# Attention and a spectral filter in one statically scheduled kernel: six exp buffers for four, longer rows of value matmuls, column-tile fillers, bf16 filter products

## The chip, the cores and the metric

The kernel runs on one core of one Trainium2 chip. Times are device microseconds (us) from the runs; a span is the time from the first to the last instruction in the trace. TensorE (PE in the profile) multiplies matrices, ScalarE (ACT) computes exponentials, VectorE (DVE) does the rest, SyncE issues transfers. PSUM is the memory that TensorE writes its results to, in eight banks; an eviction is the copy of a result out of it.

## The reference

Two independent layers on inputs of 2048 x 640, their outputs side by side:

```python
# A: spectral filter
X = rfft2(x); X = X * (w_r + 1j*w_i); a = irfft2(X)
# B: attention, 32 heads of 20
q, k, v = heads(x @ wqkv)
p = softmax(q @ k.T * 20**-0.5)
b = (p @ v) @ wo
return concatenate([a, b], axis=-1)
```

The cost is in B: 32 x 2048 x 2048 = 134 million exponentials. The kernel handles them as 2048 tiles of 128 keys by 512 queries. A unit is four heads and 512 queries: 64 tiles; there are 32 units.

## The kernel before

The program of each engine is laid out ahead of time. While the kernel is built, a loop plays through the execution with costs for every operation, and each engine that becomes free takes the first job in its own list of preferences that is ready. What comes out is a fixed order of instructions for each engine with waits on semaphores. The costs in that loop order the instructions and nothing else; on the chip only the order and the waits count. (The kernel holds a second, plain program, class `KB`, that runs only when a check at the end of the first finds its sums out of range.)

```python
def dispatch(self, e):
    if e == "pe":
        return (self.try_qk() or self.try_x_alone() or self.more_bg() or self.try_pv(4)
                or self.tail_pe() or self.try_bg_pe() or self.warm())
    if e == "act":
        if self.try_exp() or self.tail_act(): return True
        ...
    if e == "dve":
        return (self.dve_q(self.dve_urgent) or self.try_bg_ev("dve") or self.try_x_first()
                or self.try_x_step() or self.vmax())
```

- `try_qk`: score matmuls of 3 or 2 tiles, in row tiles of the array, into one of two halves of PSUM (3 + 2 banks).
- `try_exp`: ScalarE exponentiates such a group into one of four exp buffers `PT`, if that buffer is free.
- `try_pv`: value matmuls, four heads at once in column tiles, into PSUM bank 6; when all tiles of a buffer are used, it is free.
- `x`: a tile pair that VectorE exponentiates itself.
- `bg`: all other work, in PSUM banks 5 and 7: projections, out-projection, and the filter's matmuls. `try_bg_ev` moves their results out of PSUM.
- `warm`: filler matmuls of zeros, meant to keep TensorE's clock up.

Row tiles, column tiles and the whole array are the three tiling modes of TensorE. A row of value matmuls is several passes of `try_pv` one after another, with no change of mode between them.

Of the kernel before, what the change touches and what calls it, by code (L numbers as in the profile page):

```python
# [266 lines left out]
class KB:  # L267
# [805 lines left out]
    def mk_jobs_A(self, p0_after):  # L1073
# [171 lines left out]
        for ci_, (b0, n) in enumerate(chunks):  # L1245
            ne = n * 128
            flat = lambda t, c: t[:, c, b0:b0 + n, :].rearrange("p b m -> p (b m)")
            wr, wi, y0, y1 = flat(self.Wp, 0), flat(self.Wp, 1), flat(self.XY, 0), flat(self.XY, 1)
            t = [tt[:, 0:ne] for tt in self.tmp]

            def mult(k, w, ne=ne, t=t):
                def mkev(bank):
                    return lambda e, en: e.tensor_tensor(t[k], ps[:, bank, 0:ne], w, ALU.mult)  # L1253
                return (mkev, 0.0, 1.0417 * ne + 124, kw, [("tmp", k)] + zw("K", 2), [])

            def comb(y, k0, k1, op, key, t=t):
                def mkev(bank):
                    return lambda e, en: e.tensor_tensor(y, t[k0], t[k1], op)
                return (mkev, 0.0, 1.0417 * ne + 144, [("tmp", k0), ("tmp", k1), zr("K", 2)], [key] + zw("B", 3), [])
            for co in range(2):  # L1260
                pe = []
                for ti, (m, ci) in enumerate(((0, 0), (1, 1)) if co == 0 else ((0, 1), (2, 0))):
                    def mk(bank, m=m, ci=ci, b0=b0, n=n, ti=ti):
                        r_ = self.BT[:, ci, b0:b0 + n, :].rearrange("p b m -> p (b m)")
                        return lambda e: e.matmul(ps[:, bank, 0:n * 128], self.kron[:, m, :], r_, start=(ti == 0), stop=(ti == 1))
                    pe.append((mk, ne / 2.4 + 3, [("BT", ci, ci_ // 2), ("kron",), zr("A", 4)]))
                if co == 0:
                    ev = [mult(0, wr), mult(2, wi)]
                    aft = [s5[(0, ci_ // 2)], s5[(1, ci_ // 2)]] + ([s7[ci_ - 1]] if ci_ else st["S4"] + st["S2"])
                else:  # L1270
                    ev = [mult(1, wi), mult(3, wr), comb(y0, 0, 1, ALU.subtract, ("XY", 0, ci_)), comb(y1, 2, 3, ALU.add, ("XY", 1, ci_))]
                    aft = [s7[ci_]]
                s7[ci_] = self.add_job(Job("FS2_%d_%d" % (ci_, co), PRIO, pe, ev, after=aft))
                s7[ci_].ev_eng = "dve"
# [10 lines left out]
        n10 = 8 * 2 * 256  # L1285

        def s10_load(J, p, h=0):
            self.dma(self.iCS.rearrange("p s m n -> p (s m n)"), self.c_iCS.ap()[:, h * n10:(h + 1) * n10], w=[("iCS",)] + zw("K", 3), name="ld_iCS")
        J_s10l = evt("S10load", [s7[nch - 1]], s10_load, lat=8)
        st["S10"] = []  # L1290
        for h in range(2):
            if h:
                J_s10l = evt("S10load1", list(st["S10"]), lambda J, p: s10_load(J, p, 1), lat=8)
            for lt, sp in [(lt, sp) for lt in range(3) for sp in range(4 * h, 4 * h + 4)]:
                M = 128 if lt < 2 else 65
                pe = []
                for i in range(2):
                    sbv = 2 * sp + i
                    for c in range(2):
                        def mk(bank, sbv=sbv, c=c, i=i, lt=lt, M=M):  # L1300
                            o = ps[0:M, bank, i * 256:(i + 1) * 256]
                            l = self.UT[:, sbv, c, lt * 128:lt * 128 + M]
                            r_ = self.iCS[:, sbv % 8, c, :]
                            s_, e_ = (c == 0), (c == 1)
                            return lambda e: e.matmul(o, l, r_, start=s_, stop=e_)
                        pe.append((mk, 108.0, [*[("UT", c, b) for b in range(6)], ("iCS",), zr("B", 4), zr("K", 3)]))
# [8 lines left out]
        def s11_load(J, p):  # L1315
            self.dma(self.G.rearrange("p t c d -> p (t c d)"), self.c_G.ap(), w=[("G",)] + zw("K", 4), name="ld_G")
        J_s11l = evt("S11load", st["S10"], s11_load, lat=8)
        st["S11"] = []
        for sbv in range(16):
            for half in range(2):  # L1320
                pe = []
                n6 = 0
                for lt in range(3):
                    M = 128 if lt < 2 else 65
                    for c in range(2):
                        def mk(bank, lt=lt, c=c, M=M, sbv=sbv, half=half, n6=n6):
                            o = ps[:, bank, 0:320]
                            l = self.ZT[0:M, lt, sbv, c, :]
                            r_ = self.G[0:M, lt, c, half * 320:(half + 1) * 320]
# [39 lines left out]
NXV = 3  # L1369
LOG2E = 1.4426950408889634  # L1370
# [10 lines left out]
class FK(KB):  # L1381
# [8 lines left out]
    def alloc(self):  # L1390
# [12 lines left out]
        self.wq_pad = a.bf(take(10240), 5 * 8 * 128).rearrange("p (c g m) -> p c g m", c=5, g=8)  # L1403
# [3 lines left out]
        self.PT = [a.bf(take(3072 - 1024 * (i % 2)), 1536 - 512 * (i % 2)) for i in range(4)]  # L1407
# [24 lines left out]
    def zone(self, z, total):  # L1432
# [5 lines left out]
        self.spare = total - self.zK - 8192  # L1438
        assert self.zK + 8192 <= total, (self.zK + 8192, total)
# [18 lines left out]
        self.tmp = [a.f32(zK + i * 2048, 512) for i in range(4)]  # L1458
        self.iCS = a.bf(zK, 8 * 2 * 256).rearrange("p (s m n) -> p s m n", s=8, m=2)
        self.G = a.bf(zK, 3 * 2 * 640).rearrange("p (t c d) -> p t c d", t=3, c=2)  # L1460

    def setup_B(self):
# [4 lines left out]
        kq[:, 0] = kq[:, 2] = 1.0  # L1467
        kq[20::32, 0:4] = (0.0, 1.0, 0.0, Y_ROW)
        kqd = self.nc.inline_tensor(kq, self.prefix + "kq")
# [7 lines left out]
        def ldw(a, b, key):  # L1477
            self.dma(self.wqkv[:, :, a:b], wv[:, :, a:b], w=[("wqkv", key)], name="ld_w" + key)
        ldx(0)
        ldw(640, 736, "k0")  # L1480
        ldw(0, 80, "q0")
# [5 lines left out]
        ldw(80, 640, "q")  # L1487
        ldw(1360, 1920, "v")
        wq, ws, zt, va, ps, o1 = self.wq_pad, self.ws, self.zt, self.Vaug, self.ps, self.ones1
# [3 lines left out]
        wq5 = wq.rearrange("p c g (j e) -> p (c g j) e", e=32)[:, :, 20:32]  # L1493
        P.add("dve", lambda e: e.memset(wq5, 0.0), w=[("wqz",)], name="ms_wq")
# [5 lines left out]
        self.wpad("act", 0)  # L1500

    def add_row(self, e, en, out, in_, c):

# [4 lines left out]

    def wpad(self, en, g):

        src = self.wqkv[:, :, g * 80: g * 80 + 80].rearrange("p c (j d) -> p c j d", j=4)
        d4 = self.wq_pad[:, :, g, :].rearrange("p c (j e) -> p c j e", e=32)[:, :, :, 0:20]
        self.P.add(en, lambda e: copy_on(e, en, d4, src), r=[("wqkv", "q" if g else "q0"), ("z", "B", 0)], w=[("wq", g)], name="wpad")
        self.wq_done.add(g)
# [85 lines left out]
    def dummy2(self):  # L1600

        ps, k, z = self.ps, self.KT, self.zt.to_broadcast([128, 128])
        self.P.add("pe", lambda e: e.matmul(ps[:, 6, :], z, k[:, 0, 0:512], start=False, stop=False, skip_group_check=True),  # L1603
                   r=[("KT", 0, 0), ("zt",)], pw=[("ps", 6)], name="dummy")

    def job_QA(self, u):
# [3 lines left out]
        for cbv in range(5):  # L1610
            def mk(bank, cbv=cbv):
                o = ps[:, bank, :]
                l = self.wq_pad[:, cbv, g, :]
                r_ = self.xT[:, cbv, qc * 512:(qc + 1) * 512]
                st, sp = (cbv == 0), (cbv == 4)
                return lambda e: e.matmul(o, l, r_, start=st, stop=sp)  # L1616
            pe.append((mk, 216.0, [("wq", g), ("wqz",), ("xT", qc, cbv // 2)]))

        def mkev(bank):
# [3 lines left out]
        cond = lambda p: g in self.wq_done and (u < 2 or self.qk_left[u - 2] == 0)  # L1623
        return Job("QA%d" % u, 0.0, pe, ev, after=[self.sj[("xT", qc, gi)] for gi in range(3)], cond=cond,
                   minp=(0.0 if u == 0 else 21000.0))
# [98 lines left out]
    def try_exp(self):  # L1724
        i = self.nexp
        if i >= self.nqk or self.qk_t[i] > self.now or self.pt_free[i % 4] > self.now:
# [4 lines left out]
        pt = self.PT[i % 4][:, 0:512 * n]  # L1731
        in_ = self.ps[:, h:h + n, :].rearrange("p b n -> p (b n)")
        self.P.add("act", lambda e: e.activation(pt, in_, AF.Exp, scale=SCALE, bias=-15.0 / LOG2E),  # L1733
                   r=[("ps", h + k) for k in range(n)], w=[("PT", i % 4)], name="exp")
        t = self.occupy("act", 512 * n * 0.8333 + 50.0, 0.0)
        self.half_free[i % 2] = t
        self.pt_free[i % 4] = 1e18
        self.pt_left[i % 4] = n
        for k, (u, kt, j) in enumerate(tiles):
            self.pv_ready[u].append((t, kt, j, self.PT[i % 4][:, 512 * k:512 * k + 512], ("PT", i % 4)))  # L1740
# [8 lines left out]
    def next_x(self, js):  # L1749
# [28 lines left out]
        if tile[2] in js and self.x_skip < 2:  # L1778
# [6 lines left out]
    def try_x_alone(self):  # L1785
        if self.x_pair is None or (self.x_pair[0][0] >= self.u_act and self.now < self.x_at + 2500.0):
# [76 lines left out]
    def try_pv(self, least):  # L1863
# [16 lines left out]
        stuck = i < self.nqk and self.qk_t[i] <= self.now and self.pt_free[i % 4] > self.now + 1e9 and self.tf["act"] <= self.now  # L1880
        if len(pick) < (1 if stuck else min(least, heads)):
            return False

# [32 lines left out]

    def wpad_late(self, g):
        self.wpad("dve", g)
        self.occupy("dve", 350.0)
# [278 lines left out]
    def warm(self):  # L2198
# [8 lines left out]
        self.occupy("pe", self.pe_dur(216.0, "f"))  # L2207
        return True

    def dispatch(self, e):  # L2210
        if e == "pe":
            return (self.try_qk() or self.try_x_alone() or self.more_bg() or self.try_pv(4) or self.tail_pe() or self.try_bg_pe() or self.warm())
# [10 lines left out]
    def run(self):  # L2223
# [17 lines left out]
        self.pt_free = [0.0] * 4  # L2241
        self.pt_left = [0] * 4
# [47 lines left out]
        for g in range(1, NG):  # L2290
            t = 19000.0 + 2000.0 * g
            self.dve_urgent.append((t, lambda g=g: self.wpad_late(g)))
            self.at(t)
# [46 lines left out]
    def build(self):  # L2340
        self.wq_done = set()
# [7 lines left out]
def bass_concat_heads__spectral_gfnet__softmax_full_mha__prompt_kernel(  # L2349
# [11 lines left out]
    fast = FK(nc, arena, *args, cfg=dict(LEAD=20, T_A=760000.0, WARM_SHARE=0.45, RUN=2, PVQ=8, WIN=1400.0, T_X=40000.0, AHEAD=45e3, T_RB=9000.0))  # L2361
# [32 lines left out]
```

## Time and profile before

| | before |
|---|---|
| time, median of the first three runs | 877.55 us (876.75 to 877.59) |
| ScalarE, VectorE, TensorE busy | 95%, 90%, 92% of the span |
| exp groups on ScalarE, polynomial tiles on VectorE | 724, 238 |
| ScalarE idle before exps | 18.8 us |
| VectorE busy from 40 to 820 us | 729.4 of 780 us |

"Idle before, releaser" in a group's row is the time in which the engine stood still just before these instructions and what ended most of it. The prediction below shows the rows for ScalarE. It does not show who kept VectorE waiting while it might have computed polynomials (waits of VectorE from 40 to 830 us: us in total, times, longest):

```profile
DVE arena L1807 <- PE ps L1716: 20.4, 28, 1.4
DVE arena L1507 <- PE ps L1616: 4.3, 5, 1.9
DVE arena L1507 <- PE ps L1548: 3.7, 3, 1.8
DVE arena L227 <- PE ps L1983: 3.3, 2, 1.8
```

L1807 is the polynomial's first step, waiting for its score tile (L1716); the other rows are evictions of query projections, key projections and out-projections. The loop gives VectorE any job that is ready, so a long wait at an eviction suggests that no polynomial step was ready when the order was laid out; it does not prove it, as on the chip the order is fixed.

### The profile page before, as it was taken

To read this page: it belongs to the slowest core of one execution; us is meant where nothing else is said; L and a number is where in the kernel's file an instruction comes from. 1 tells how busy PE (TensorE), PEld (TensorE's weight loads), DVE (VectorE), ACT (ScalarE), POOL (GpSimd) and SP (SyncE) were. 2 spreads that over 40 slices of the span, in tenths; PEclk is the share of its full clock that TensorE was granted. 3 is DMA by queue.
4 is the path that set the end of the run, shared out by engine and by line. 5 is a ranking of instruction groups with operands and counts; after the bars stand their busy time and mean duration, and the time that the engine had idled before them with its cause. 6 is when DMAs were issued, how large, how long until landed. Compare 5 with 4: busy or idle time off the path is not lost.

```text
span 875.8 us, 16211 instructions
## 1 busy us (share of the span) xinstructions
PE 804.7 (92%) x6687; PEld 285.9 (33%) x6772; DVE 785.9 (90%) x1495; ACT 835.2 (95%) x740; POOL 2.9 (0%) x7
## 2 busy tenths in 40 slices
PE   8999999999889999999899988999999999999986
PEld 4433333334233333322233422222333333323322
DVE  3487799999998799999999899999999989999993
ACT  6999999999999899999999999999999999999993
POOL 1000000000000000000000000000000000000000
PEclk9999999999999999999999999999999999999999
DMA  8430000000311000010100000001001120111101
GB/s 239 95 82 14 2 13 14 14 13 3 139 46 37 21 13 2 14 49 14 49 13 30 19 10 14 13 13 51 13 13 63 36 58 11 43 43 44 44 14 33
DMA packets 31972, 31.83 MB, mean 36 GB/s; under 512 B 13588, under 2 KB 26644, under 8 KB 31636
## 3 DMA queue, kind: packets, MB, share of 16 engines
q1 hardware_dynamic: 31892, 30.73, 11.6%
q8 instruction: 54, 0.88, 0.4%
q14 instruction: 26, 0.21, 0.1%
HBM read 24.97 MB, written 5.50 MB: 35 GB/s over the span
## 4 chain that ended last, share of the span: by engine, by line
ACT 55%; DVE 26%; PE 16%; issue 1%; DMA 0%; SPq 0%; ACTq 0%; DVEq 0%
ACT arena L1733 55%; PE ps L1716 5%; DVE arena L227 5%; DVE arena L1807 4%; PE ps L1899 3%; DVE arena L1507 2%; DVE arena L1847 2%; DVE arena L1851 2%; DVE arena L1854 2%; DVE arena L1253 2%; PE ps L1983 1%; DVE arena L2186 1%; DVE arena L1845 1%; DVE arena L1843 1%; DVE arena L1849 1%
## 5 line engine op out<-in xcount | busy, mean ns | idle before, releaser
L1733 ACT ACTIVATE arena<-ps 128x1536 bf16<-128x1536 f32 x724 | 826.0, 1277 | 18.8 <-PE ps L1716 9.3
L1716 PE MATMUL ps<-arena 32*128 32x512 bf16 x2048 | 303.8, 384 | 47.3 <-ACT arena L1733 33.2
L1899 PE MATMUL ps<-arena 128*32 128x512 bf16 (+3 forms) x2048 | 203.1, 390 | 2.9 <-DVE arena L1923 1.7
L1807 DVE TENSOR_SCALAR arena<-ps 128x512 uint16<-128x512 f32 x238 | 163.1, 685 | 21.6 <-PE ps L1716 20.4
L1716 PEld LDWEIGHTS ps<-arena 32*128 32x128 bf16 x2048 | 74.8, 91 | 250.2 <-ACT arena L1733 199.9
L227 DVE CAST arena<-ps 128x320 bf16<-128x320 f32 (+4 forms) x190 | 103.7, 546 | 16.7 <-PE ps L1576 10.1
L1899 PEld LDWEIGHTS ps<-arena 128*32 128x32 bf16 (+1 forms) x2048 | 51.0, 92 | 124.4 <-issue 102.4
L1847 DVE TENSOR_TENSOR arena<-arena 128x1024 f16<-128x1024 uint16 x119 | 81.4, 686 | 1.3
L1851 DVE TENSOR_TENSOR arena<-arena 128x1024 f16<-128x1024 f16 x119 | 81.6, 685 | 1.2
L1854 DVE TENSOR_TENSOR arena<-arena 128x1024 uint16<-128x1024 uint16 x119 | 81.3, 684 | 0.6
L1603 PE MATMUL ps<-arena 128*128 128x512 bf16 x205 | 68.6, 387 | 2.5 <-issue 1.4
L1507 DVE TENSOR_SCALAR arena<-ps,arena 128x512 bf16<-128x512 f32 x62 | 50.0, 806 | 14.1 <-PE ps L1548 9.6
L1849 DVE TENSOR_SCALAR arena<-arena 128x1024 f16<-128x1024 uint16 x119 | 50.2, 422 | 1.1
L1845 DVE TENSOR_SCALAR arena<-arena 128x1024 f16<-128x1024 uint16 x119 | 49.9, 421 | 1.1
L1843 DVE TENSOR_SCALAR arena<-arena 128x1024 uint16<-128x1024 uint16 x119 | 50.0, 423 | 0.6
L1548 PE MATMUL ps<-arena 128*32 128x512 bf16 x640 | 47.3, 381 | 1.6 <-DVE arena L1807 0.8
L227 DVE COPY arena<-ps 128x1024 bf16<-128x1024 bf16 (+2 forms) x55 | 40.1, 732 | 9.4 <-PE ps L540 6.8
L1616 PE MATMUL ps<-arena 128*128 128x512 bf16 x143 | 43.2, 383 | 1.7 <-DVE arena L1507 0.6
L1331 PE MATMUL ps<-arena 128*128 128x320 bf16 (+1 forms) x192 | 38.4, 303 | 0.3 <-DVE arena L227 0.2
L1983 PE MATMUL ps<-arena 128*128 128x320 bf16 x192 | 36.8, 302 | 0.4 <-issue 0.2
L1576 PE MATMUL ps<-arena 128*128 128x80 bf16 (+1 forms) x320 | 33.2, 236 | 0.7 <-DVE arena L1807 0.3
L1603 PEld LDWEIGHTS ps<-arena 128*128 128x128 bf16 x266 | 21.5, 97 | 34.9 <-issue 30.0
(69 smaller groups left out, 442.7 us busy)
## 6 DMA issues: line engine op xcount, KB each, us to landing
arena<-rscr SPq DMA_DIRECT2D x31, 256.0 KB
arena<-in_B_x_dram SPq DMA_DIRECT2D x4, 640.0 KB, 6.4
arena<-in_A_x_dram SPq DMA_DIRECT2D x4, 640.0 KB, 5.8
out_dram<-arena SPq DMA_DIRECT2D x16, 160.0 KB, 1.8
out_dram<-arena SPq DMA_DIRECT2D x4, 640.0 KB, 3.2
arena<-f_ciCS SPq DMA_DIRECT2D x2, 1024.0 KB, 5.2
arena<-arena SPq DMA_DIRECT2D x124, 2.0 KB, 1.7
arena<-f_cslab SPq DMA_DIRECT2D x2, 768.0 KB, 4.3
```

The source lines that it names most:

```text
L227: return eng.tensor_copy(out, in_)
L1507: return e.tensor_scalar(out, in_, m, b, ALU.mult, ALU.add)
L1603: self.P.add("pe", lambda e: e.matmul(ps[:, 6, :], z, k[:, 0, 0:512], start=False, stop=False, skip_group_check=True), r=[("KT", 0, 0), (" ...
L1716: inst = e.matmul(ps[:, bank, :], kt_[32 * j:32 * j + 32, g, kt * 128:(kt + 1) * 128], q[32 * j:32 * j + 32, :], start=True, stop=True, ti ...
L1733: self.P.add("act", lambda e: e.activation(pt, in_, AF.Exp, scale=SCALE, bias=-15.0 / LOG2E), r=[("ps", h + k) for k in range(n)], w=[("PT ...
L1807: self.P.add("dve", lambda e: e.tensor_scalar(v, in_, 1024.0 * SCALE * LOG2E, 31743.0, ALU.mult, ALU.min), r=[("ps", bank)], **({"w": [key ...
L1843: t = self.x_op(n, one, lambda e: e.tensor_single_scalar(sh, v, 6, ALU.logical_shift_left), [kv], [ka], "x_s")
L1847: t = self.x_op(n, two, lambda e: e.tensor_tensor(b16, sh, b16, ALU.mult), [ka, kb], [kb], "x_q")
L1849: t = self.x_op(n, one, lambda e: e.tensor_scalar(a16, sh, -4.0 * X_B / 65536.0, -4.0 * X_A, ALU.mult, ALU.add), [ka], [ka], "x_l")
L1851: t = self.x_op(n, two, lambda e: e.tensor_tensor(b16, b16, a16, ALU.mult), [ka, kb], [kb], "x_h")
L1854: t = self.x_op(n, two, lambda e: e.tensor_tensor(v, v, b16, ALU.add), [kb, kv], [kv], "x_w")
L1899: inst = e.matmul(ps[32 * j:32 * j + m, 6, :], va[:, kt, 21 * h:21 * h + m], pt, start=st, stop=sp, tile_position=(0, 32 * j))
```

## The change

Its intent: ScalarE should no longer wait for a free exp buffer (six buffers; several other tables shrink to make room for them), TensorE should change its tiling mode less often (value matmuls in rows, column tiles also for query projections and fillers), and VectorE should get time for more polynomial tiles (filter products in bf16, no copies of the query weights, lone polynomial tiles issued at once).

```diff
+NPT = 6
-        self.PT = [... for i in range(4)]
+        self.PT = [... for i in range(NPT)]
-        self.wq_pad = a.bf(take(10240), 5 * 8 * 128)...      # zero-padded copy of the query weights
+        self.wq = a.bf(take(6560), 5 * 656)...               # the weights as loaded
-        self.tmp = [a.f32(zK + i * 2048, 512) for i in range(4)]
+        self.tmp = [a.bf(zK + i * 1024, 512) for i in range(4)]
 ... iCS in eight pieces through three slots, G in two halves
-                return lambda e: e.matmul(o, l, r_, start=st, stop=sp)          # query projection
+                    for j in range(4):
+                        i = e.matmul(ps[32*j:32*j+32, bank, :], self.wq[:, cbv, c:c+32], r_, ..., tile_position=(0, 32*j))
 ... dummy2 (filler): the whole array after a whole-array matmul, else four column tiles
-        if tile[2] in js and self.x_skip < 2:
+        if tile[2] in js and self.x_skip < self.cfg["SKIP"]:
-        ... self.now < self.x_at + 2500.0
+        ... self.now < self.x_at + self.cfg["ALONE"]
 # try_pv
+        if self.mode != "c" and self.pv_left[u] > self.cfg["PVB"] and len(lst) < self.cfg["PVB"]:
+            if sum(t > self.now for t in self.pt_free) < self.cfg["PTB"]:
+                return False
 # dispatch, TensorE
-            return (self.try_qk() or self.try_x_alone() or ...
+            return (self.try_qk() or (self.mode == "c" and self.try_pv(4)) or self.try_x_alone() or ...
-    cfg=dict(LEAD=20, T_A=760000.0, ..., RUN=2, PVQ=8, ...)
+    cfg=dict(LEAD=28, T_A=600000.0, ..., RUN=1, PVQ=6, ..., SKIP=1, ALONE=0.0, PVB=12, PTB=5)
```

`PVB` and `PTB`: unless TensorE is in column tiles already, a value pass waits until 12 tiles are ready or five buffers are in use. `SKIP` and `ALONE`: how often and how long a lone polynomial tile waits for a score pass to join. `T_A`, `RUN` and `PVQ` pace the background work.

## The prediction

> **What bounds the kernel now.** I read the page first (busy shares and slices), then each engine's waits, then busy time in stretches of 25 us, then the timeline of 20 us in the middle. From the page, parts 1 and 5 (columns of part 5: line, engine, operation, count | busy us, mean ns | idle before, releaser):
>
> ```profile
> span 875.8 us, 16211 instructions
> PE 804.7 (92%) x6687; PEld 285.9 (33%) x6772; DVE 785.9 (90%) x1495; ACT 835.2 (95%) x740; POOL 2.9 (0%) x7
> ...
> L1733 ACT ACTIVATE arena<-ps 128x1536 bf16<-128x1536 f32 x724 | 826.0, 1277 | 18.8 <-PE ps L1716 9.3
> ...
> L1807 DVE TENSOR_SCALAR arena<-ps 128x512 uint16<-128x512 f32 x238 | 163.1, 685 | 21.6 <-PE ps L1716 20.4
> ```
>
> The 2048 score tiles of 128x512 are exponentiated in two places. ScalarE takes 724 groups, alternately of 3 and 2 tiles: 724 x 2.5 = 1810. VectorE takes the other 238 (the count of L1807) with a nine-instruction polynomial for each pair. ScalarE is the bound: from its first exp at 14.6 us to its last at about 859 it is idle for 18.8 us only; the tail after it (out-projection of the last unit) takes 17 us. In unbroken stretches the chain of waits shows an exp group every 1.135 us (66 groups in 74.94 us), 0.455 us a tile. So 724 groups cost 823 us at the least, and 14.6 + 823 + 17 = 855 is the floor for this division of tiles.
>
> The stretches of 25 us (from:to, length, then busy us and instructions of PE, weight load, DVE, ACT, POOL) show that in the middle VectorE is as full as ScalarE:
>
> ```profile
> 75.00:100.00 25.00, 23.59 (x259) 9.84 (x260) 18.31 (x32) 21.94 (x20) 0.00 (x0) 1.00 0.04 12
> ...
> 275.00:300.00 25.00, 23.62 (x200) 9.74 (x202) 18.18 (x33) 21.68 (x20) 0.00 (x0) 1.00 0.10 32
> ...
> 375.00:400.00 25.00, 22.95 (x176) 7.64 (x176) 24.90 (x52) 25.00 (x23) 0.00 (x0) 1.00 0.14 43
> ```
>
> 375 to 400 us is the normal case: both at 99% or more, nothing to win by removing waits. The first two rows are the exceptions, where both starve together. Adding up what VectorE lacks of full in such stretches between 40 and 850 us gives 50 us (18 of it before 125 us); for ScalarE between 25 and 850 it is 18 us.
>
> Who lets ScalarE wait (waits of ACT, 20 to 860 us: us, times, longest):
>
> ```profile
> ACT arena L1733 <- PE ps L1716: 8.8, 12, 3.3
> ACT arena L1733 <- PE ps L1899: 7.8, 16, 0.9
> ```
>
> L1716 is the score matmul coming late; L1899 is the value matmul, which has not yet freed an exp buffer. The second is just what two more buffers are for.
>
> **What the Trainium skill says.** "TensorEngine Tiling (Array Packing)", section Key Properties: changing the tiling mode drains TensorE. The trace agrees in size. Scores use row tiles, values column tiles, everything else the whole array; the timeline at 402 us has
>
> ```profile
> 403.06 0.39 PE L1716 MATMUL ps<-arena 32*128 32x512 bf16 x3 [0.22 <-ACT arena L1733]
> ...
> 403.38 0.40 PE L1899 MATMUL ps<-arena 128*32 128x512 bf16 x4
> ...
> 403.71 0.31 PE L1198 MATMUL ps<-arena 128*128 128x328 bf16 x1
> ```
>
> Starts lie 0.32 us apart across a change of mode, while five column-tile passes in a row take 1.25 us (20 matmuls of L1548 at 90.05), about 0.21 from one to the next: a switch costs 0.11 us. "VectorE: DVE Perf Modes", section What auto-detection actually checks: a two-source op does two elements a cycle only if every tensor is 16-bit. The trace agrees: the filter's combination with f32 inputs (L1258) takes 682 ns median for 512 elements, the bf16/f16 tensor-tensor ops of the polynomial 685 ns for 1024. "ScalarE: Activation LUTs", section What ACT_TABLE_LOAD costs, gives 0.833 ns an element for every function; 1280 elements are then 1067 ns, and the 1135 measured leaves 68 ns a group. So nothing in this change can make one exp cheaper; only fewer tiles or fewer gaps count.
>
> **The change part by part.**
> 1. *Filter products in bf16.* The 44 products read PSUM and stay near 652 ns. The 20 full-size combinations of 22 fall from 682 to about 350 ns (half of the 1024-element op): 20 x 0.33 = 6.6 us of VectorE.
> 2. *Query weights used directly in column tiles.* Seven copies of 275 ns (1.9 us) and most of a 0.86 us memset leave VectorE, mostly before 33 us, where it idles anyway. One 0.52 us copy leaves ScalarE at 7.6 us, where it waits for x anyway. The 160 query matmuls become 640 in quarters, the same five passes of 0.21 us. Against the end: 1 us at most. Parts 1 and 2 give VectorE 8 to 9 us.
> 3. *Six exp buffers.* Aimed at the 7.8 us of waits for L1899 (16 times). Each such wait also breaks the back-to-back overlap. I expect 6 to 7 us back.
> 4. *Value matmuls in longer rows.* Now every value pass stands alone between two mode changes (all ten of those I looked at from 400 to 412 us). 2048 / 4 = 512 passes; in rows of three, about 340 visits fewer, one switch saved at each: 340 x 0.11 = 37 us of TensorE. Column-tile fillers and query projections save some more. TensorE is no bound at 400 us, where fillers (L1603, 205 of them) use its slack, but before 125 us it is. So scores come earlier there: of the 8.8 us of L1716 waits I expect 4 to 5 back. The 3.3 us one at 284 us is a query projection standing behind out-projections, and the change leaves that priority alone.
> 5. *Polynomial tiles issued alone at once* (wait 2.5 us -> 0, skips 2 -> 1). Aimed at the 20.4 us that VectorE waits at L1807. It costs a score pass and up to two switches more for each lone tile; part 4 pays for it.
> 6. *Tables in pieces, filter paced to 600 rather than 760.* The transfers ran beside other work and still do; the second table of the last stage adds one load of some 8 us in which no filter job runs, filled by polynomial tiles. Filter work moves earlier (its last stage starts at 727 us now), total unchanged.
>
> **The sum.** Let R be the VectorE time won and G the gain. A polynomial tile costs VectorE 2.08 us (790 to 850 us: busy 58.9, less some 10 of other work, over 23.5 tiles) and takes 0.455 from ScalarE. VectorE also loses G of its own time when the kernel shortens: n = (R - G) / 2.08 extra tiles, G = W + 0.455 n, with W the ScalarE idling removed. I take W = 11 (parts 3 and 4) and R = 9 + 30 = 39 (60% of the 50 us of idling; a choice, since the schedule is built greedily and part of the idling is the dependence between filter stages). Then 1.219 G = 11 + 0.219 x 39 = 19.5, G = 16, n = 11: 877.5 - 16 = 861.5, rounded to 862.
>
> **Rivals.** (a) *Everything is recovered*: W = 19, R = 59 gives G = 26, 851 us. For it: the saturated stretches show both engines can stay at 99%; against: the starving at the start comes from transfers and projections that remain. (b) *The ScalarE waits only change their name*: there are still only two halves of score banks, so the exp of a group waits for a score pass that must fit in about 1.1 us; a row of three value passes (0.65 us plus switches) just ahead of it makes L1716 waits out of L1899 waits. Then W = 4, R = 19, G = 6.7: 871 us. For it: L1716 is already the larger releaser. (c) *TensorE becomes the bound* while the filter is squeezed to an earlier end and lone polynomial tiles add passes; its busy share is 92%. Against: over a fifth of the passes that it makes beside scores and values at 400 us are fillers. That would be 875 to 885 us. (d) *The tables' pieces stall the filter and the end slips*: unlikely, as the filter ends at 828 us now and is moved earlier.
>
> **Range and chances.** (a) and (b) bound what I think likely: 851 to 872 holds 8 in 10. The 2% line lies at 860, just below my middle, so faster by over 2% gets 0.42, within 2% 0.56, slower (only (c) at its worst) 0.02.
>
> **What would show it.** Exp groups 724 -> about 720, L1807 238 -> about 249; idle before exps 18.8 -> about 8 us, with L1899 nearly gone as a releaser; the combination near 350 ns; value passes in rows of three or more at 0.21 us; VectorE at 92 to 93% of the span; last filter matmul near 690 us; the tail still 17 us. I am wrong if L1716 waits of ScalarE grow (rival b), if VectorE's 50 us of idling stay, or if the time falls though the number of exp groups and the idle before them do not.

## More of the kernel before

Which tiles the polynomial takes depends on `LEAD`:

```python
u = self.u_act                                # the unit whose scores are being issued
if len(self.rem[u]) < self.cfg["LEAD"]:       # few tiles of it are left:
    u += 1                                    # take one of the next unit
if u >= 32 or u > self.u_pv + 1:
    return None
free = [(kt, j) for kt, j in self.rem[u] if self.scores_ready(u, kt)]   # queries and keys there?
```

## The result

The changed kernel takes 866.38 us (median of 4 runs, 865.83 to 866.52), the kernel before 877.45 beside it. The ratio is 0.9874 (95% interval 0.9857 to 0.9891), a gain of 1.3%. Ratios here and below are the mean time of one kernel's fast runs over that of the other's fast runs in the same rounds, so not quite the ratio of the medians quoted. The middle of the prediction was 862; the result lies within its range.

The page of the changed kernel, parts 1 and 5 (L1751 is the exp, L1734 the score matmul, L1825 the polynomial's first step):

```profile
span 862.5 us, 18266 instructions
...
PE 791.6 (92%) x7750; PEld 274.6 (32%) x7783; DVE 764.9 (89%) x1472; ACT 832.0 (96%) x741; POOL 2.9 (0%) x7
...
L1751 ACT ACTIVATE arena<-ps 128x1536 bf16<-128x1536 f32 x726 | 823.3, 1365 | 7.4 <-PE ps L1734 6.6
...
L1825 DVE TENSOR_SCALAR arena<-ps 128x512 uint16<-128x512 f32 x234 | 159.3, 684 | 10.7 <-PE ps L1734 9.9
```

Idle before exps fell from 18.8 to 7.4 us, and the value matmul is gone as a releaser. The number of exps did not fall: 726 groups where there were 724, and 234 polynomial tiles where there were 238. So ScalarE does slightly more and waits much less. The waits of ScalarE from 20 to 846 us (us, times, longest), all of them:

```profile
ACT arena L1751 <- PE ps L1734: 6.1, 13, 1.1
```

Where the time went, from the first to the last exp of each trace: 844.3 us before (14.6 to 858.9), 830.2 after (15.4 to 845.5), 14.1 less. Of that 11.4 are idle time taken away. Two groups more cost 2 x 1.134 = 2.3. The rest is pace: stream less idle inside it, divided by the groups, is (844.3 - 18.3) / 724 = 1.141 us before and (830.2 - 6.9) / 726 = 1.134 after, 5.0 us over the stream. The pace goes with the number of breaks, however short: ScalarE stood idle 55 times in the stream before and 26 times after. In all traces it is 1.140 to 1.143 with four buffers (52 to 72 breaks) and 1.132 to 1.135 with six (13 to 31 breaks), e2 below with its 24 us of idling included. That a break costs the overlap of an exp with its predecessor is the likely reason. 11.4 - 2.3 + 5.0 = 14.1. The tail after the last exp is 17 us in both.

The stretches of 25 us that the prediction showed, now in the changed kernel (from:to, length, busy us and instructions of PE, weight load, DVE, ACT, POOL):

```profile
75.00:100.00 25.00, 24.45 (x274) 10.26 (x272) 14.31 (x25) 23.41 (x22) 0.00 (x0) 1.00 0.04 12
275.00:300.00 25.00, 22.24 (x260) 9.13 (x257) 22.80 (x44) 24.57 (x23) 0.00 (x0) 1.00 0.06 19
375.00:400.00 25.00, 22.89 (x220) 7.03 (x218) 24.03 (x49) 25.00 (x23) 0.00 (x0) 1.00 0.14 44
```

ScalarE gained in the first two, but VectorE, fuller from 275 us on, is emptier from 75 to 100 us than it was, 14.3 against 18.3, and no longer quite full at 375. From 40 to 820 us it is busy for 728.1 of 780 us, against 729.4: it idles as much as before, although it has less to do. Its waits from 40 to 830 us (us in total, times, longest), as shown for the kernel before:

```profile
DVE arena L227 <- PE ps L2000: 10.1, 7, 2.6
DVE arena L1825 <- PE ps L1734: 9.9, 15, 1.8
DVE arena L1514 <- PE ps L1548: 8.0, 6, 2.1
DVE arena L1514 <- PE ps L1630: 6.8, 4, 2.0
DVE arena L227 <- PE ps L1576: 5.8, 7, 1.6
```

The wait at the polynomial's first step was halved, 20.4 to 9.9. But the waits of evictions (L1514 of key and query projections, L227 after L2000 of out-projections and after L1576 of value projections) grew by more, from 11.3 us in the rows shown to 30.7: VectorE now stands before an eviction, by all appearances with no polynomial tile in hand. Why it has none is what the experiments had to find.

### The profile page after: what moved, and what is told of

Same layout as the page of the kernel before. It is cut to its first block, busy times and chain, and to the rows that moved or that the text cites. A ratio compares the mean times of both kernels' runs of the same rounds, so it can differ in the third digit from the quotient of the medians.

```text
span 862.5 us, 18266 instructions
## 1 busy us (share of the span) xinstructions
PE 791.6 (92%) x7750; PEld 274.6 (32%) x7783; DVE 764.9 (89%) x1472; ACT 832.0 (96%) x741; POOL 2.9 (0%) x7
## 4 chain that ended last, share of the span: by engine, by line
ACT 57%; DVE 29%; PE 12%; issue 1%; ACTq 0%; DVEq 0%
ACT arena L1751 57%; DVE arena L1825 5%; DVE arena L227 5%; PE ps L1734 3%; DVE arena L1253 3%; DVE arena L1514 3%; DVE arena L1865 2%; DVE arena L1872 2%; DVE arena L1869 2%; PE ps L1920 2%; DVE arena L2203 1%; DVE arena L1863 1%; PE ps L1548 1%; DVE arena L1861 1%; DVE arena L1867 1%; PE ps L2000 1%
## 5 line engine op out<-in xcount | busy, mean ns | idle before, releaser
L1751 ACT ACTIVATE arena<-ps 128x1536 bf16<-128x1536 f32 x726 | 823.3, 1365 | 7.4 <-PE ps L1734 6.6
L1734 PE MATMUL ps<-arena 32*128 32x512 bf16 x2048 | 313.0, 384 | 45.3 <-ACT arena L1751 29.1
L1920 PE MATMUL ps<-arena 128*32 128x512 bf16 (+3 forms) x2048 | 188.4, 385 | 2.5 <-ACT arena L1751 0.9
L1825 DVE TENSOR_SCALAR arena<-ps 128x512 uint16<-128x512 f32 x234 | 159.3, 684 | 10.7 <-PE ps L1734 9.9
L1734 PEld LDWEIGHTS ps<-arena 32*128 32x128 bf16 x2048 | 77.6, 91 | 285.9 <-ACT arena L1751 211.6
L227 DVE CAST arena<-ps 128x320 bf16<-128x320 f32 (+3 forms) x190 | 103.9, 547 | 27.2 <-PE ps L1576 13.9
L1869 DVE TENSOR_TENSOR arena<-arena 128x1024 f16<-128x1024 f16 x117 | 80.4, 688 | 0.6
L1872 DVE TENSOR_TENSOR arena<-arena 128x1024 uint16<-128x1024 uint16 x117 | 79.9, 684 | 0.4
L1614 PE MATMUL ps<-arena 128*32 128x512 bf16 x760 | 72.8, 387 | 0.5 <-DVE arena L1940 0.5
L1514 DVE TENSOR_SCALAR arena<-ps,arena 128x512 bf16<-128x512 f32 x62 | 50.0, 806 | 23.0 <-PE ps L1548 16.2
L1920 PEld LDWEIGHTS ps<-arena 128*32 128x32 bf16 (+1 forms) x2048 | 46.0, 93 | 70.5 <-issue 57.2
L1548 PE MATMUL ps<-arena 128*32 128x512 bf16 x640 | 52.8, 384 | 0.8 <-ACT arena L226 0.3
L1630 PE MATMUL ps<-arena 128*32 128x512 bf16 x640 | 49.3, 382 | 0.4 <-DVE arena L227 0.3
L1867 DVE TENSOR_SCALAR arena<-arena 128x1024 f16<-128x1024 uint16 x117 | 49.0, 419 | 0.4
L227 DVE COPY arena<-ps 128x1024 bf16<-128x1024 bf16 (+2 forms) x55 | 40.1, 731 | 9.1 <-PE ps L540 7.9
L2000 PE MATMUL ps<-arena 128*128 128x320 bf16 x192 | 35.8, 302 | 0.0
L1170 PE MATMUL ps<-arena 128*128 128x328 bf16 x160 | 31.6, 306 | 0.7 <-DVE arena L227 0.7
L1576 PE MATMUL ps<-arena 128*128 128x80 bf16 (+1 forms) x320 | 31.2, 236 | 0.0
```

Source lines behind the costliest of these rows:

```text
L227: return eng.tensor_copy(out, in_)
L1514: return e.tensor_scalar(out, in_, m, b, ALU.mult, ALU.add)
L1548: inst = e.matmul(ps[32 * j:32 * j + 32, bank, :], self.wqkv[:, cbv, c:c + 32], r_, start=st, stop=sp, tile_position=(0, 32 * j))
L1614: i = e.matmul(ps[32 * j:32 * j + 32, 6, :], z, k, start=False, stop=False, skip_group_check=True, tile_position=(0, 32 * j))
L1734: inst = e.matmul(ps[:, bank, :], kt_[32 * j:32 * j + 32, g, kt * 128:(kt + 1) * 128], q[32 * j:32 * j + 32, :], start=True, stop=True, ti ...
L1751: self.P.add("act", lambda e: e.activation(pt, in_, AF.Exp, scale=SCALE, bias=-15.0 / LOG2E), r=[("ps", h + k) for k in range(n)], w=[("PT ...
```

## The experiments

They ran in three batches of three rounds (five for e6), each on a chip of its own with the kernel before in the same rounds: e1 to e4 (before: 877.24 us), then e5, e6, e8, e9 (876.99), then c1, e7, e10, e11 (876.79). Every run is a program of its own, laid out anew by the loop, so an edit also shifts what it does not name. Counts of exp groups and polynomial tiles are fixed when a program is built, so they could be written into what was expected.

My theory at the start: the gain is ScalarE's waiting, taken away mainly by the buffers, which the longer rows need; the higher `LEAD` pays for it with VectorE's idling. Rivals: TensorE's relief alone makes the gain; or the choice of polynomial tiles does.

### e1: four buffers

```diff
-NPT = 6
+NPT = 4
-PTB=5
+PTB=3
```

> The changed kernel with four exp buffers instead of six (and three instead of five of them in use before a short value row may start); all else as changed. Its program has 723 exp groups and 242 polynomial tiles. My theory: the two extra buffers carry most of the gain, and the longer value rows even need them, so ScalarE's waits for the value matmul come back at 10 us or more, total idle before exps above 20 us, and the time is 880 to 888 us, at or above the kernel before. Rival (rows, column-tile fillers and query projections relieve TensorE, the buffers add little): idle before exps stays under 10 us and the time within 3 us of 866.

Measured: 885.67 us (ratio to before 1.0099, 1.0082 to 1.0116), idle before exps 26.4 us. Waits of ScalarE from 20 us to the last exp:

```profile
ACT arena L1751 <- PE ps L1920: 14.0, 28, 1.5
ACT arena L1751 <- PE ps L1734: 9.4, 8, 2.5
```

As expected: everything else of the change with four buffers is slower than the kernel before. The waits for the value matmul (L1920) are many and short.

### e2: no longer rows

```diff
-            return (self.try_qk() or (self.mode == "c" and self.try_pv(4)) or self.try_x_alone() ...
+            return (self.try_qk() or self.try_x_alone() ...
-PVB=12
+PVB=0
```

> The changed kernel without the two rules that lengthen value rows (no waiting for 12 ready tiles, no value pass ahead of fillers); six buffers kept. 724 exp groups, 238 polynomial tiles as in the kernel before. My theory: about half of the gain goes, 870 to 874 us, with ScalarE's waits for the value matmul near zero (buffers) but its waits for the score matmul back at 8 us or more. Rival A (buffers alone make the gain): within 2 us of 866. Rival B (rows alone make it): 876 to 878.

Measured: 878.43 us (1.0014, 0.9997 to 1.0030), idle 24.7 us. My theory missed, and rival B's number (876 to 878) all but came in. But the profile does not look like either story:

```profile
ACT arena L1751 <- PE ps L1920: 12.7, 3, 8.5
ACT arena L1751 <- PE ps L1734: 11.2, 14, 2.2
```

The waits for value matmuls did not vanish: three, one of them 8.5 us long (another of 3.9). Six buffers were full, once for 8.5 us. Something held the value matmuls themselves back.

### e3: the old threshold

```diff
-LEAD=28
+LEAD=20
```

> The changed kernel with polynomial tiles taken from the next unit only when fewer than 20 (not 28) score tiles of the current one are left. 720 exp groups and 248 polynomial tiles, 14 more than in the change. My theory: the higher threshold pays for freedom of ScalarE from waits with VectorE idling; so VectorE idles some 10 us less, but idle before exps rises to 15 us or more and the time is 868 to 876. Rival (the threshold alone is what kept the polynomial tiles from growing, at no gain): idle before exps stays below 9 us and the time falls to 858 to 862.

Measured: 873.75 us (0.9964, 0.9947 to 0.9981), idle 23.4 us, with 14 polynomial tiles more than the change. As I expected in numbers, and again with one long stop:

```profile
ACT arena L1751 <- PE ps L1920: 12.3, 1, 12.3
ACT arena L1751 <- PE ps L1734: 10.2, 14, 3.1
```

VectorE, from 40 to 820 us, is busy for 11.8 us more than in the change (columns as above), so it idles for 40.1 us instead of 51.9:

```profile
40.00:820.00 780.00, 723.30 (x7057) 242.64 (x7049) 739.91 (x1432) 758.21 (x670) 0.00 (x0) 1.00 0.10 28
```

The timeline of VectorE during that stop (start, length, engine, line, operation; L1253, L1258 and L227 are the filter, L1867, L1869 and L1872 the last three steps of a polynomial pair, L1940 the copy of the finished unit out of PSUM):

```profile
542.75 0.42 DVE L1867 TENSOR_SCALAR arena<-arena 128x1024 f16<-128x1024 uint16 x1
...
543.54 1.42 DVE L1253 TENSOR_TENSOR arena<-ps,arena 128x512 bf16<-128x512 f32 x2
544.87 0.88 DVE L1258 TENSOR_TENSOR arena<-arena 128x512 bf16<-128x512 bf16 x2
545.67 0.68 DVE L227 CAST arena<-ps 128x512 bf16<-128x512 f32 x1
546.27 0.68 DVE L1869 TENSOR_TENSOR arena<-arena 128x1024 f16<-128x1024 f16 x1
547.05 1.42 DVE L1253 TENSOR_TENSOR arena<-ps,arena 128x512 bf16<-128x512 f32 x2
548.38 0.68 DVE L227 CAST arena<-ps 128x512 bf16<-128x512 f32 x1
548.98 0.68 DVE L1872 TENSOR_TENSOR arena<-arena 128x1024 uint16<-128x1024 uint16 x1
549.77 1.42 DVE L1253 TENSOR_TENSOR arena<-ps,arena 128x512 bf16<-128x512 f32 x2
...
551.89 0.68 DVE L1940 COPY arena<-ps 128x512 f32<-128x512 f32 x1
```

Three steps of the last pair of a unit, 1.8 us of work, take from 542.75 to 549.66, because evictions and products of the filter stand in between. Bank 6 cannot be emptied until this pair's value matmul is done, so all exps of the next unit stay in their buffers, the six fill up, and ScalarE stops from 540.8 to 553.1. That is a new theory: a late pair, not a lack of buffers, made the long stops of e2 and e3, and `LEAD=28` protects against it by taking the polynomial tiles of a unit earlier (that it protected by design or by chance is not shown: e2, at 28, has such stops too).

### e4: lone tiles wait again

```diff
-SKIP=1, ALONE=0.0
+SKIP=2, ALONE=2500.0
```

> The changed kernel with the old rule for lone polynomial tiles (two skips, 2.5 us wait). 732 exp groups and 218 polynomial tiles. My theory: idle before exps stays under 9 us, ScalarE has 6 groups more at 1.133 us, and the time is 872 to 875; VectorE's waits for score matmuls rise from 10 to over 20 us. Rival (lone tiles cost TensorE as much as they give): 866 or less.

Measured: 867.51 us (0.9892, 0.9875 to 0.9908), idle 6.1 us; VectorE waits at the polynomial's first step for 27.0 us. Every count came out as I said, the time did not: 1.6 us above the changed kernel in its second measurement, where 6 groups more should cost 6.8. The stream of exps is 834.5 us long against 830.2: 6.8 more for the groups, 1.3 less idle, 1.2 less by pace. The first exp of this trace happened to start at 14.0 us instead of 15.4 (c1 below, the same program as the change, has 14.1), and about 2 us of the changed kernel's time lie outside its span (c1). Lone issue is worth 4.3 us in the stream of exps, of which 1.6 show in the time.

### e5: e3, with late pairs first

```diff
-LEAD=28
+LEAD=20
+    def x_late(self):
+        u = self.u_pv
+        return u < 32 and len(self.rem[u]) <= 0 and any(c[3][0][0] == u for c in self.x_run)
-            return (self.dve_q(self.dve_urgent) or self.try_bg_ev("dve") or ...
+            return (self.dve_q(self.dve_urgent) or (self.x_late() and self.try_x_step()) or self.try_bg_ev("dve") or ...
```

> As e3 (threshold 20), with one rule added on VectorE: once all score tiles of the unit whose values are being summed are issued, the polynomial steps go ahead of filter evictions. 722 exp groups, 244 polynomial tiles. In e3 ScalarE stood still once for 12.3 us, at 541 to 553 us, while VectorE did eleven filter operations between the steps of the last polynomial pair of a unit. My theory: that order made the stall; it falls below 3 us, idle before exps to 10 to 13 us, and the time to 863 to 868. Rival (the stall comes from exp buffers or TensorE, and VectorE's order is innocent): one stall of 8 us or more stays and the time is 871 to 876.

Measured: 863.82 us (0.9851, 0.9836 to 0.9867), idle 13.6 us, of which one wait of 1.4 us is for a value matmul. Nothing but the order of VectorE's instructions and what follows from it differs from e3, and the long stop is gone with 10 us. The rival falls. The tiles stay: 244, ten more than in the change, with VectorE idling for 40.7 us from 40 to 820 us.

### e9: e2, with late pairs first

The edits of e2 and the rule of e5, at `LEAD=28`.

> As e2 (six buffers, no rules for longer value rows), with the same rule on VectorE. 726 exp groups, 234 polynomial tiles. If e2's loss of 12 us was mostly the two stalls of 8.5 and 3.9 us behind late polynomial pairs, and not the shorter rows as such, idle before exps falls from 24.7 to 11 to 14 us and the time to 869 to 873, the rows being worth some 4 us. Rival (the rows themselves carry the gain): idle before exps stays above 20 us and the time at 877 or more.

Measured: 870.45 us (0.9927, 0.9912 to 0.9942), idle 13.3 us. All waits of ScalarE for value matmuls are gone; for the score matmul they are

```profile
ACT arena L1751 <- PE ps L1734: 12.5, 16, 2.2
```

So of the 12.5 us that e2 lost to the changed kernel (878.43 against 865.88), about 8 were the late pairs and 4.6 (870.45 - 865.88) the rows as such. e2 read by itself would have credited the rows with the whole gain.

### e6: only the bf16 products, in the order of before

```diff
-        self.tmp = [a.f32(zK + i * 2048, 512) for i in range(4)]
+        self.tmp = [a.bf(zK + i * 1024, 512) for i in range(4)]
```

This is an edit of the kernel before; the cost in the schedule was left alone so that every engine keeps its order.

> The kernel before with only the filter products stored in bf16; every engine has the same instructions in the same order as before. 20 combinations fall from 682 to 416 ns, 5.3 us of VectorE. My theory: with the order fixed VectorE idles for what it saves, as ScalarE sets the pace: within 1 us of the kernel before (ratio 0.999 to 1.001). Rival (VectorE is an equal bound where the filter runs, 509 to 595 us): 2 to 5 us faster.

Measured: 875.92 us, five runs, against 876.99 (0.9990, 0.9977 to 1.0004). VectorE's busy time falls by 5.0 us to 780.9, idle before exps by 1.8 us to 17.0, and the interval includes no change at all. Time saved on VectorE is worth 1 us or so by itself (2 at most, by the interval) when the order does not also hand it more tiles.

### c1: the changed kernel again

> The changed kernel itself, unaltered, on the chip of the experiments. Its first four runs lasted 3.7 to 4.0 us longer than their spans in the trace, all other kernels 1.6 to 1.9 us. If that belongs to the program, 866 us and 3.7 us or more between time and span; if to the place of those first runs (my guess), 864 to 865 us with less than 2.2 us between.

Measured: 865.88 us (0.9877, 0.9860 to 0.9893), and time less span is 3.4 to 4.2 us in its four runs. My guess was wrong: it belongs to this program. In all other kernels, the kernel before included, the difference is 1.6 to 1.9 us. So about 2 us of what the change gains within its span (13.3 us) are lost outside it. I found no cause; it stays open. It also blurs comparisons with the changed kernel by time. By their median spans (862.2 us for c1) e4 is 3.5 us slower than the change, e7 4.7, e9 6.7 and e10 20.9, each about 2 us more than the times say; e5, 2.1 us faster by time, has the same span (862.1); and e11 is 6.9 us shorter instead of 8.8.

### e7: fillers over the whole array

```diff
-        if self.mode == "f":
+        if True:
             z = self.zt.to_broadcast([128, 128])
...
-        self.occupy("pe", self.pe_dur(216.0, "f" if self.mode == "f" else "c"))
+        self.occupy("pe", self.pe_dur(216.0, "f"))
```

> The changed kernel with fillers over the whole array only, as before. 725 exp groups, 236 polynomial tiles; 1718 mode changes in its program against 1647. If column-tile fillers matter, 71 mode changes of 0.11 us are 8 us of TensorE, part of which reaches ScalarE: idle before exps 11 to 15 us, 868 to 871 us. Rival (fillers only use TensorE's slack): within 1.5 us of the changed kernel.

Measured: 868.71 us (0.9906, 0.9890 to 0.9923), idle 14.9 us, 13.7 of it for the score matmul. The mechanism is as expected, and the amount (2.8 us over c1) at its lower edge. Fillers are not free: when they change TensorE's mode, scores come late.

### e10: four buffers, with late pairs first

The edits of e1 and the rule of e5.

> As e1 (four exp buffers), with the VectorE rule of e5. 723 exp groups, 242 polynomial tiles. e1's waits for value matmuls were 28 of at most 1.5 us, not one long one, so my theory: late pairs are not their cause, idle before exps stays above 20 us and the time at 880 to 887 us, which leaves the number of buffers as the cause. Rival (e1 suffered from late pairs like e2 and e3): idle falls below 15 us and the time below 874.

Measured: 884.89 us (1.0093, 1.0076 to 1.0110), idle 26.3 us:

```profile
ACT arena L1751 <- PE ps L1924: 13.5, 25, 1.8
ACT arena L1751 <- PE ps L1734: 9.8, 9, 2.5
```

The waits for value matmuls (L1924 here) stay many and short. Late pairs are not the cause in e1; the number of buffers is. The two buffers are worth 19 us with the rest of the change in place, more than the whole gain. That waiting for twelve ready tiles costs space to keep them in may be why; no run has four buffers without that rule, so it is not shown.

### e8 and e11: versions meant to beat both

A first form of e8 was refused before it reached a chip: with another fallback for the choice of tiles a filter job still held PSUM bank 5 when the tail wrote there. It was dropped. What ran is the change with

```diff
-LEAD=28                                              +LEAD=24 (e8), 26 (e11); 16 in the last unit
-out-projections ahead of query projections            +query projections ahead
+the VectorE rule of e5 (in e11 from 4 unissued tiles on)
-MODE = 100.0, SLACK = 200.0                           +90.0; 100.0 (e8), 150.0 (e11)
-PVB=12                                               +16 (e11)
```

> A version meant to beat both: the changed kernel with the VectorE rule of e5, threshold 24 (16 in the last unit), query projections ahead of out-projections, and the schedule's own costs for a mode switch and for the slack after a VectorE write cut from 100 and 200 ns to 90 and 100. 718 exp groups, 254 polynomial tiles (726 and 234 in the change). My theory: 8 groups less are 9 us of ScalarE; if idle before exps stays at 7 to 12 us, the time is 856 to 862. Rival (more polynomial tiles bring back late pairs and stalls): idle above 18 us, 866 or more.

Measured for e8: 860.83 us (0.9820, 0.9805 to 0.9835), idle 12.8 us: within what was expected for the time, and just above it for the idle.

> A second try at beating both: as e8 but with threshold 26, value rows waiting for 16 tiles, the VectorE rule from 4 unissued score tiles on, and a slack of 150 ns. 719 exp groups, 252 polynomial tiles. Expected 859 to 863 us, idle before exps 11 to 14 us, as e8; above 866 the tuned values of e8 would be an accident of its schedule.

Measured for e11: 857.07 us (0.9774, 0.9758 to 0.9791), below what I expected, idle 8.5 us. Its page:

```profile
PE 794.9 (93%) x7788; PEld 277.5 (32%) x7788; DVE 796.8 (93%) x1544; ACT 824.0 (96%) x734; POOL 2.9 (0%) x7
...
L1751 ACT ACTIVATE arena<-ps 128x1536 bf16<-128x1536 f32 x719 | 815.3, 1353 | 8.5 <-PE ps L1734 7.5
```

Here VectorE is busy for 759.0 of the 780 us from 40 to 820, 31 us more than in the change, and 252 tiles are polynomial. Seven groups less than the change are 7.9 us, and the span is 6.5 us shorter. This version beats both kernels, by 2.3% over the one before and 1.0% over the change (857.07 against 865.88 beside it; clear of noise). Both were picked from many built variants by what their schedules promised and then measured; how much each setting contributes was not taken apart.

## Why the prediction was right or wrong

**The bound and W: right.** ScalarE's stream sets the end, and the idle before exps fell by 11.4 us where I took 11. The parts were split a little differently. The 7.8 us behind value matmuls vanished altogether (6 to 7 expected); of the 8.8 us behind score matmuls 2.7 came back, not 4 to 5. e1 and e10 show that the buffers carry the first; e7 and e9 show that fillers and rows carry the second (without either, ScalarE waits some 13 us for scores). Rival (b), waits that change their name, is what happens in e7 and e9, but not in the change as a whole. That the overlap of exps would bring 5.0 us more in pace was mentioned for the waits, but is not a term of the sum. Of the other rivals, (a), all waits recovered, came true for a good half of ScalarE's 19 us and for none of VectorE's 50; (c) did not happen, as ScalarE waits less for TensorE than before; nor did (d), as the filter ends at 826 us. Two small slips of the working change nothing: the polynomial has eight instructions for a pair, not nine (two reads of PSUM and six more), and 724 groups at 74.94 / 66 us are 822 us, not 823.

**R and n: wrong; this is the step that failed.** "60% of the 50 us of idling" should have turned into 11 more polynomial tiles. None of it did: VectorE idles for 52 us between 40 and 820 us where it idled for 51, and there are 4 tiles fewer, not 11 more. The prediction had named this as a sign that it is wrong ("if VectorE's 50 us of idling stay"). I did not weigh `LEAD` 20 -> 28, the smallest line of the diff; it had no part of its own in the working. With 28, polynomial tiles come from the next unit from halfway through the current one, and that unit's queries and keys are often not there yet. Playing the schedule through again by its own costs (not a measurement), VectorE stands idle for lack of ready scores of the next unit for 7 us before and 25 us after (a second count, by a slightly different rule, gives 10, 27, and 14 for the change at 20), and in the last unit, which has no next, it stops taking tiles at 28 instead of 20. On the chip, e3 and e5 with 20 have 248 and 244 tiles, 10 and 6 more than before, and VectorE idles for 40 and 41 us instead of 52. So the rest of the change does bring most of the 11 tiles, and this line took them back. Even then only some 10 of the 30 us of idling are won; e8 and e11, with other settings as well, win 30. e3 also shows what 28 buys: without it a late pair stops ScalarE for 12.3 us. e5 shows that the same safety is to be had from an order of work, and e8 and e11 that the tiles are then there, with VectorE at 93%: the figure I had predicted for the change itself.

**The sum.** In place of G = 11 + 0.455 x 11 = 16 stand 11.4 of idle, minus 2.3 for two groups more, plus 5.0 of pace: 14.1 in the stream, 13.3 in the span, and 11.1 in the time (877.45 - 866.38), since the changed program takes 2 us more outside its span. The miss of 4.9 us against the unrounded 861.5 is 5.0 of tiles that did not move, 2.3 of groups added, 0.8 of a later first exp and 2.2 outside the span, less 5.0 of pace and 0.4 of idling. So it is partly luck that the result lies this near the middle: the gain in pace, which the sum lacked, hid the tiles that did not move.

**Sizes within the parts.** Part 1: the combination takes

```profile
L1258 DVE TENSOR_TENSOR arena<-arena x22: 215/416/426, 519.3 to 601.1; 128x512 bf16<-128x512 bf16 x20, 128x128 bf16<-128x128 bf16 x2
```

416 ns median (min/median/max are shown), not 350. I halved 685, which halves its fixed part as well. "VectorE: DVE Perf Modes", the breakdown Side-by-side: where the cycles go, has a fixed part of about 150 cycles for an operation, and the trace agrees: 416 ns for 512 elements and 685 for 1024 leave 416 - (685 - 416) = 147 ns fixed, 141 cycles at the page's 0.96 GHz. 20 x 0.266 = 5.3 us, not 6.6; and in e6 they reach the end by 1 us (2 at most). Part 4: value rows did not come in threes. In the built program the value passes form 432 visits where they formed 499; never more than two stand together, since a score pass cuts in. Mode changes fall from 1870 to 1647. At 0.11 us that is 25 us of TensorE instead of 37. The row rules account for most of these 223 changes (built without them, e2 and e9 have 1779 and 1799), fillers in column tiles for 71 (e7); the shares overlap, as a filler or a query projection often stands beside a value pass, as here in the changed kernel (L1614 a filler in column tiles, L1920 the value pass):

```profile
400.59 0.39 PE L1734 MATMUL ps<-arena 32*128 32x512 bf16 x3 [0.31 <-ACT arena L1751]
400.91 0.40 PE L1614 MATMUL ps<-arena 128*32 128x512 bf16 x4
401.14 0.39 PE L1920 MATMUL ps<-arena 128*32 128x512 bf16 x4
```

0.32 us from score to filler across a mode change, 0.23 from filler to value pass without one. Part 6: "filter work moves earlier" was wrong. The last filter matmul starts at 826.2 us, against 827.8 before. The pace setting does not bind: the changed kernel built with 760 has the same instructions in the same order on every engine as with 600. Part 5 halved the waits it aimed at, and e4 puts its worth at 1.6 us in time, 3.5 in span. The column-tile query projections without copies (part 2) and the tables in pieces (part 6) were not taken back alone, so their shares are not shown.

**The chances** of 0.56 for within 2% and 0.42 for faster stood on a middle of 862; with n at its measured value the same sum gives W = 11 minus 1.8 for four tiles, 868, and would have left little doubt.

## What to carry to other kernels

In a kernel laid out by a greedy loop, time saved on an engine can become idling, as here, when the loop has nothing ready to put there; look at what makes the next job eligible before counting on it, and at the smallest constants of a diff first. When all buffers are full, look for what keeps the oldest one from being emptied: it may be one short chain that stands behind low-value work in another engine's queue, and a change of order (e5, e9) may end it without another buffer. Undoing one part alone can create an accident of the schedule that is larger than the part; look at the number and length of the waits (one of 12.3 us, or 28 of 0.5) before giving the part the credit.

## What the Trainium skill lacked or had wrong

- "TensorEngine Tiling (Array Packing)", Key Properties, says that a change of tiling mode drains TensorE, without a cost. Here it is about 0.11 us (0.32 us between starts across a change, 0.21 within a mode), and 71 changes more moved the time by 2.8 us and the span by 4.7 (e7 against c1).
- "ScalarE: Activation LUTs", What ACT_TABLE_LOAD costs, gives 0.833 ns an element, which fits (1280 elements are 1067 ns of the 1134 that a group takes), and says that back-to-back operations overlap by about 93 ns. It does not say what a break in the stream costs besides its own length. Here 29 breaks fewer (55 before, 26 after) went with 5.0 us of pace, by estimate 0.17 us each, more than the page's overlap.
- No page has it: the changed program takes 3.4 to 4.2 us more than its span in eight runs, all other programs here 1.6 to 1.9. The cause is open.
